# A local and summary attention with mixed experts on one core: band mask in three forms, key maxima in fp16 steps, copies between tiles also as transfers, a new written-out order

## The chip, the cores and the metric

One core of a Trainium2 chip runs the whole program. The time is device time in microseconds for one execution; a lower time is better. Results come as the median over runs, and one further execution was profiled.

## The reference

Two stages follow each other. The first is an attention in which each position sees its neighbours within 15 places and, beside them, 24 summaries of the whole sequence: per block of 32 positions the maximum of the keys and the mean of the values. The second takes the first one's output as `x` and runs four experts, each a causal attention of its own with a projection behind it, mixed by the two strongest gates of each position.

```python
B, H, S, D = q.shape                       # 4, 8, 768, 64
block, window = (32, 16)
k_sum = k.reshape(B, H, nb, block, D).max(axis=3)
v_sum = v.reshape(B, H, nb, block, D).mean(axis=3)
scores_l = scale * np.matmul(q, k.transpose(0, 1, 3, 2))
mask_l = np.abs(pos[:, None] - pos[None, :]) < window
scores_s = scale * np.einsum('bhsd,bhnd->bhsn', q, k_sum)
scores_s = scores_s + np.log(block)
scores_l_m = np.where(mask_l, scores_l, -1000000000.0)
...
a = a / (np.sum(a, axis=-1, keepdims=True) + 1e-09)
v_all = np.concatenate([v, v_sum], axis=2)
return np.matmul(a, v_all).astype(np.float32)
```

```python
logits = x @ w_gate                        # x: (4, 768, 512)
...
for e in range(E):                         # 4 experts, width 64
    q = x @ wq[e]
    k = x @ wk[e]
    v = x @ wv[e]
    ...
    ye = a @ v @ wo[e]                     # a: causal softmax
    for kk in range(K):                    # the 2 strongest gates
        mask = topk[:, :, kk] == e
        out += mask[..., None] * w[:, :, kk:kk + 1] * ye
```

## The kernel before

The work is a list of small steps. `make_plan` makes the list: each step has a name, the buffers it reads and writes, and a function that issues its instructions. `TABLE` holds the order: one entry per step with its number, its engine (V VectorE, A ScalarE, G GpSimd, S SyncE, P TensorE) and the slots of the buffers that it is first to use. `Plan.emit` walks through the table and issues the steps, so the order on each engine's queue is the table's order read for that engine. An engine works through its queue in order: a step that waits holds all behind it. The costs beside each step ("V": 0.95 and so on) and the `dma` figures belong to the planner that made the table; they have no part in the execution. The names in this document are those of the steps, with the batch first, then the head pair or expert pair, then a part: `sc031` is batch 0, head pair 3, half 1.

**Loads.** `dk`/`dq` bring keys and queries of four heads, cast to fp16, on GpSimd's queue; batch 0's first four heads come in two parts. `dv` brings the values of a head pair into `vb` (fp32, 25 tiles of 64 rows, shifted by 16 places) on SyncE's or ScalarE's queue. `vb` has six slots, so later loads wait until earlier head pairs are through.

**Value rows.** A band tile needs 96 rows, 64 own ones and 32 of the next tile. `hc` copies those 32 rows from partitions 0..31 to 64..95 within the tile (L166 or L164, the shared copy helpers). `vq` handles the ends of a head: it copies the last 16 rows and zeroes the first 16 of the next head (L288). `vz` and part of `vone` zero rows and ones once, at the start. `ds` copies the 24 value means, one copy for each of the 12 tiles of a head, into rows 96..119.

**Means.** For batch 0 and some groups `bs` sums with matmuls (L306) and `be` takes the sums out on VectorE (L324). For the groups in `TREE` a second load `dvs` (four DMAs on SyncE, L341) brings the values into `vt`, and `tr` adds them in five steps on GpSimd (L355). `vtz` clears `vt` once ahead of this (L238).

**First stage, per head pair.** `tk`, `tq` transpose keys and queries on TensorE (L373), `kw` lays the keys out in 12 overlapping tiles, `rk` takes the block maxima with one reduction on VectorE (L393), `ksc` copies them into each tile, `cq` takes the queries out. `sc` opens each half with the band mask, a matmul of `mt` with `pi` for each of two heads (L426), and adds the scores (L432). `ex` is the exponential on ScalarE (L440), `av` the matmuls with `vb` (L450), `rc` (L461) and `xm` (L465) divide, `tx` transposes (L477), `hi` and `lo` (L495) split the result into two fp16 parts.

**Second stage, per batch.** `pp` projects (L640), `pc` takes it out, `vp` gives expert values and gates (L570, L573), `lg`/`v2` take them out, `ga`, `gx`, `gb`, `gc` make the gates, `sp` the scores (L664), `es` the exponentials (L672), `dm` the causal cut of diagonal blocks on GpSimd (L677), `aw` the matmuls with the values (L688), `r2` and `wv` weight them, `tw` and `ct` transpose them, `op` projects out (L750), `oc` copies to `ob`, `od` stores (L766). `dw`, `dwv`, `dwo`, `dwg` load weights, `cw`, `cvg`, `cg`, `co` cast them. `f` entries of the table are matmuls on zeros (L773) without any use for the result.

Of the kernel before, what the change touches and what calls it, by code (L numbers as in the profile page):

```python
# [8 lines left out]
HALF = mybir.dt.float16  # L9
# [16 lines left out]
TREE = {(1, 1), (2, 0), (2, 1), (3, 0), (3, 1)}  # L26
# [26 lines left out]
4,V, 18,S,0 10,G, 8,V, 17,V, 0,V, f,P,0.8 7,V, 112,S, 20,A, 13,G,0 15,G, 14,G,0 16,G, 30,G,1 11,G, 1,G, 61,P,1  # L53
5,V, 62,A,0 63,V,0 44,P,0 64,V, 45,A,1 f,P,2.5 31,G,1 78,P,0 79,A,2 9,G, 2,G, 3,V, 46,V,0 65,P,2 48,P,3 99,P,0
204,G,0 49,V,0 82,P,1 66,A,1 24,S,1 19,V, 205,G,2 47,A, 32,S,2 21,P,3 80,V,0 22,V,0 6,G, 52,P,4 83,A,2 81,A,
50,P,1 53,A,0 95,P,6 100,A,0 246,P,7 51,A,1 96,V,1 97,V,0 26,V, 98,G, 229,P,3 67,P,4 68,A,2 25,G, 224,S,0 69,P,0
250,P,2 251,V,1 84,P,4 70,A,3 230,A,0 23,G, 216,G,0 86,P,0 33,G, 27,P,6 28,V,1 87,A,4 247,A,2 85,A,5 248,V,0
34,A, 55,P,0 231,V,1 54,P, 29,G, 56,V,0 103,P,4 104,A,1 35,P,6 71,P,4 57,V,0 36,V,1 38,S,3 39,G, 58,P,0 59,V,0
37,A, 120,G, 60,V,0 72,P, 73,V,0 74,V,0 89,P,6 88,P, 40,A, 101,P,0 102,A,5 41,P,4 280,P,5 90,V,0 91,V,1 42,V,1
43,V, 232,A, 281,A,1 249,G, 254,P,0 255,A,4 252,P,6 92,P,2 93,A,1 206,S,4 209,S,0 233,P,4 234,V,1 116,S,0 115,S,  # L60
117,S,1 225,G, 94,V,1 263,P,5 113,S, 105,P,0 211,A, 106,P, 253,A,5 107,V,0 108,V,1 235,P,2 236,A,1 114,A, 75,P,6
109,P,0 110,V,2 111,V,2 76,A,3 210,G, 208,G, 207,G, 77,V,3 221,S,2 212,P,2 213,V,1 122,G, 264,A,2 166,P,3
168,P,0 217,G,2 119,A, 167,A,0 226,G,0 218,S,3 12,G, 121,A, 169,V,1 227,G, 127,P,6 129,V,0 179,P,0 180,A,0
282,V,1 128,V,0 265,V,0 182,P,2 183,A, 130,P,4 132,A, 124,P,0 214,G, 125,A, 385,S,0 283,V, 131,V, 126,A, 176,P,2
170,P,6 171,A, 267,P,4 139,P,0 133,V,5.0 134,A, 177,A, 223,V, 268,V,0 140,V,2 228,G, 237,P,6 284,P,4 238,A,3
215,G, 266,G, 285,V,1 269,P,2 173,P,0 270,A,2 172,G, 240,P,6 135,V, 136,V,0 239,P, 174,A, 271,P,2 272,A,1 118,S,
123,A, 185,P,0 137,P,4 286,P,2 186,A, 287,A,3 241,V,0 242,V,1 243,P,6 288,P,0 138,V,0 150,P,4 222,V, 289,A,0
257,P,2 244,V,0 245,V,0 151,A,1 220,G, 144,P,0 378,G,2 256,P, 258,V,0 259,V,1 377,G,0 424,P,4 425,V,1 145,A,
386,G, 403,P,5 404,A,1 379,A,0 290,P,0 291,P, 156,P,4 157,A, 147,P,2 260,P,6 261,A,1 390,G,1 219,G, 181,G,
274,P,4 273,P, 148,A, 184,G, 292,V,0 293,V,0 262,V,1 153,P,0 154,A, 275,V,0 276,V,1 187,G, 565,G,1 294,P,2  # L70
295,A,2 632,P,6 296,V,2 387,G,0 392,S,1 437,P,7 277,P,4 278,A,3 149,G, 146,G, 155,G, 279,V,3 420,P,0 407,P,1
559,S,0 566,S,3 421,V,2 438,A,0 408,A,0 339,P,2 340,A,1 341,P,4 178,G, 388,G, 391,G,2 158,G, 175,G, 141,P,2
633,A,2 190,P,0 188,P, 342,A,0 189,P, 346,P,4 422,V,0 423,G, 352,P,6 564,G,0 389,V,2 405,V,0 380,G, 142,A,
191,V,0 192,V,0 406,V, 300,P,2 347,A,0 143,G, 303,P,4 382,A, 301,A,0 302,V,1 381,G, 152,G, 193,P,0 353,A, 305,A,
# [80 lines left out]
def make_plan(nc, T, q, k, v, moe_w_gate, moe_wq, moe_wk, moe_wv, moe_wo, out):  # L155
# [18 lines left out]
    def pbank16(b):  # L174
        return T["ps16"][:, b.slot, :]

    id16, id32, rid, mt, pi = st("id16"), st("id32"), st("rid"), st("mt"), st("pi")
    vones, vz, kwpad, v2one, knpad = st("vones"), st("vz"), st("kwpad"), st("v2one"), st("knpad")
    wqk, wvg, wo = [st("wqk0"), st("wqk1")], st("wvg"), st("wo")

    def id16s(e):
# [753 lines left out]
```

## Time and profile before

| what | us |
|---|---|
| median of 3 runs | 178.65 |
| the three runs | 178.45, 178.65, 183.42 |
| the profiled execution | 177.54 |
| its span, first to last instruction | 175.8 |
| mean granted TensorE clock | 0.956 |
| SyncE waiting to issue an output store behind ScalarE, 5 times | 48.5 |
| GpSimd waiting for exponentials before `dm`, 11 times | 25.1 |

The engines are PE (TensorE's matmuls), PEld (its weight loads, which overlap), DVE (VectorE), ACT (ScalarE), POOL (GpSimd) and SP (SyncE). A row of the groups by line names the line, the engine, the operation, its output and input tile with partitions x elements, the count, then the busy us and mean ns of one, then the idle time of the engine just before, with what ended it. A row of the timeline gives the start and length in us, and in brackets how long the engine was idle before and who released it. The chain of waits follows back from the last instruction to what released each step. Matmuls are pipelined, so the busy time of one is longer than its pitch. The DMA share counts overlapping packets and can exceed 1.

### The profile page before, as it was taken

To read this page: it belongs to the slowest core of one execution; us is meant where nothing else is said; L and a number is where in the kernel's file an instruction comes from. 1 tells how busy PE (TensorE), PEld (TensorE's weight loads), DVE (VectorE), ACT (ScalarE), POOL (GpSimd) and SP (SyncE) were. 2 spreads that over 40 slices of the span, in tenths; PEclk is the share of its full clock that TensorE was granted. 3 is DMA by queue.
4 is the path that set the end of the run, shared out by engine and by line. 5 is a ranking of instruction groups with operands and counts; after the bars stand their busy time and mean duration, and the time that the engine had idled before them with its cause. 6 is when DMAs were issued, how large, how long until landed. Compare 5 with 4: busy or idle time off the path is not lost.

```text
span 175.8 us, 6926 instructions
## 1 busy us (share of the span) xinstructions
PE 148.6 (85%) x3005; PEld 108.8 (62%) x3005; DVE 122.7 (70%) x244; ACT 124.9 (71%) x160; POOL 104.9 (60%) x181
## 2 busy tenths in 40 slices
PE   0667973999896999999998899869999999999760
PEld 0236752798764777867755488648765875675420
DVE  6345566579795987799985788872896986277630
ACT  2344686169948986899687977868989583969650
POOL 8962059746965798379959999927978200324100
PEclk9995699579999999999999999999999999999998
DMA  5999999999998699999969938991001502101846
GB/s 94 181 195 198 216 186 148 152 201 193 153 197 228 80 170 188 173 194 171 150 106 175 181 55 191 250 248 49 4 4 62 183 4 75 44 4 35 300 157 229
DMA packets 44894, 25.60 MB, mean 146 GB/s; under 512 B 33344, under 2 KB 39744, under 8 KB 44864
## 3 DMA queue, kind: packets, MB, share of 16 engines
q1 hardware_dynamic: 33200, 16.08, 47.7%
q0 software_dynamic: 6432, 6.29, 23.5%
q10 hardware_dynamic: 5232, 2.79, 7.7%
q8 instruction: 23, 0.38, 1.0%
q14 instruction: 7, 0.06, 0.1%
HBM read 25.16 MB, written 6.29 MB: 179 GB/s over the span
## 4 chain that ended last, share of the span: by engine, by line
PE 42%; DMA 24%; ACT 10%; POOL 8%; DVE 7%; issue 6%; POOLq 0%; ACTq 0%; DVEq 0%
DMA vb<-in_v_dram 11%; PE ps L450 9%; DMA kn<-in_k_dram 8%; PE ps L640 6%; DMA qn<-in_q_dram 5%; PE ps L570 4%; PE ps L688 4%; ACT a L672 3%; PE ps L664 3%; PE ps L750 3%; PE ps L477 3%; PE ps L373 3%; POOL vb L166 3%; PE ps L306 2%; PE ps L426 2%
## 5 line engine op out<-in xcount | busy, mean ns | idle before, releaser
L672 ACT ACTIVATE a<-ps 128x1024 f16<-128x1024 f32 (+1 forms) x48 | 42.5, 922 | 5.6 <-PE ps L664 4.0
L677 POOL TENSOR_SCALAR_AFFINE_SELECT a<-a 128x256 f16<-128x256 f16 x48 | 19.1, 421 | 28.4 <-ACT a L672 25.1
L440 ACT ACTIVATE aT<-ps 120x768 f32<-120x768 f32 x32 | 25.4, 815 | 9.1 <-PE ps L432 6.9
L450 PE MATMUL ps<-vb,aT 120*64 120x65 f32 x768 | 28.1, 231 | 3.3 <-issue 2.3
L450 PEld LDWEIGHTS ps<-vb,aT 120*64 120x64 f32 x768 | 25.6, 145 | 6.4 <-issue 4.0
L355 POOL TENSOR_TENSOR vt<-vt 120x1024 f32<-120x1024 f32 (+3 forms) x20 | 24.1, 1205 | 1.0
L640 PE MATMUL ps<-hi,wqk 128*128 128x384 f16 x128 | 22.6, 326 | 0.4 <-DVE lo L495 0.3
L166 POOL COPY vb<-vb 16x128 f32<-16x128 f32 (+1 forms) x20 | 14.1, 712 | 9.7 <-DMA vb<-in_v_dram 8.9
L164 ACT COPY kw<-ps 128x1152 f16<-128x1152 f16 x13 | 14.4, 1122 | 7.5 <-PE ps L373 7.5
L393 DVE TENSOR_REDUCE ks<-kw 128x24 f16<-128x768 f16 x16 | 14.9, 943 | 4.8 <-ACT kw L164 4.5
L640 PEld LDWEIGHTS <-wqk 128*128 128x128 f16 x128 | 11.9, 97 | 8.4 <-issue 1.2
L664 PE MATMUL ps<-qk,qk 64*128 64x512 f16 (+3 forms) x128 | 15.8, 307 | 1.0 <-DVE wT L166 0.7
L570 PE MATMUL ps<-wvg,hi 128*128 128x264 f16 x96 | 13.9, 275 | 3.0 <-ACT a L672 1.5
L465 DVE TENSOR_TENSOR x<-ps,rec 128x768 f32<-128x768 f32 x16 | 15.3, 958 | 1.0 <-PE ps L477 0.5
L495 DVE TENSOR_TENSOR lo<-ps,hi 128x768 f16<-128x768 f32 x16 | 15.0, 955 | 1.5 <-ACT hi L164 1.0
L166 POOL COPY vb<-vu 24x768 f32<-24x768 f32 x18 | 14.8, 823 | 1.0
L688 PE MATMUL ps<-v,a 128*128 128x65 f16 x336 | 12.3, 194 | 0.6 <-POOL a L677 0.6
L688 PEld LDWEIGHTS <-a 128*128 128x128 f16 x336 | 11.2, 97 | 2.3 <-issue 0.9
L750 PE MATMUL ps<-wo,wT 128*128 128x512 f16 x48 | 12.0, 380 | 0.5 <-DVE wT L166 0.5
L432 PEld LDWEIGHTS <-kw 64*128 64x128 f16 x384 | 10.4, 98 | 2.8 <-issue 0.7
L426 PE MATMUL ps<-pi,mt 64*128 64x384 f16 x64 | 11.4, 345 | 0.3 <-DVE qT L166 0.3
L432 PE MATMUL ps<-qT,kw 64*128 64x64 f16 x384 | 11.5, 195 | 0.0
(106 smaller groups left out, 269.7 us busy)
## 6 DMA issues: line engine op xcount, KB each, us to landing
vb<-in_v_dram SPq DMA_DIRECT2D x12, 400.0 KB
out_dram<-ob SPq DMA_DIRECT2D x8, 512.0 KB
vt<-in_v_dram SPq DMA_DIRECT2D x20, 192.0 KB
kn<-in_k_dram POOLq DMA_DIRECT2D x7, 384.0 KB, 7.6
qn<-in_q_dram POOLq DMA_DIRECT2D x7, 384.0 KB, 6.3
out_dram<-ob ACTq DMA_DIRECT2D x3, 512.0 KB
vb<-in_v_dram ACTq DMA_DIRECT2D x2, 400.0 KB
vb<-in_v_dram SPq DMA_DIRECT2D x2, 384.0 KB
```

The lines of the kernel that those rows point to most:

```text
L166: en(e).tensor_copy(dst, src)
L355: en(e).tensor_tensor(y, p, q_, AL.add)
L432: nc.tensor.matmul(s[:, hp, 64 * t:64 * t + 64], T["kw"][kw.slot][r, tt, :], T["qT"][qT.slot][r].rearrange("c (s p) -> c s p", s=8)[:, :, ...
L440: nc.scalar.activation(T["aT"][aT.slot][0:KR], pbank(sc, 2)[0:KR, :, 0:384], AF.Exp, scale=SCALE)
L450: nc.tensor.matmul(pbank(av, 2)[o:o + 64, u, 65 * (2 * (t // 2) + hp):65 * (2 * (t // 2) + hp) + 65], a[0:KR, hp, 64 * t:64 * t + 64], T[" ...
L570: nc.tensor.matmul(p[:, i, 0:264], hi_(ch)[:, cols], T["wvg"][:, ch, :], start=(ch == 0), stop=False, skip_group_check=True)
L640: nc.tensor.matmul(pbank(pp, 2)[:, u, 0:384], T["wqk"][:, cc, ch, j, :], hi_(ch)[:, 384 * u:384 * u + 384], start=(ch == 0), stop=(ch == N ...
L664: nc.tensor.matmul(pbank(sp, 2)[:, ep, c0:c0 + w], T["qk"][qk[1].slot][r, 128 * tj:128 * tj + 128], T["qk"][qk[0].slot][r, n0:n0 + w], sta ...
L672: nc.scalar.activation(a2v(u), pbank(sp, 2)[:, :, 0:ln], AF.Exp, scale=SCALE / (XS * XS))
L677: nc.gpsimd.affine_select(m, m, [[0, 2], [1, 128]], AL.is_ge, 0.0, base=0, channel_multiplier=-1)
L688: nc.tensor.matmul(pbank(av, 2)[:, ep, 65 * ti:65 * ti + 65], a2v(u)[:, ep, o:o + 128], T["v2"][v2.slot][:, tj, 2 * cc + ep, :], start=(tj ...
L750: nc.tensor.matmul(pbank(op, i1 - i0)[:, ti - i0, :], T["wT"][wTs[cc].slot][:, 128 * ti:128 * ti + 128], T["wo"][:, cc, :], start=(cc == 0 ...
```

## The change

**Ends of a head.** `vz` and `vq` go, and with them the zeroing in `vone`. The mask tile `mt` gets three forms: the plain band, one with the first 16 columns blocked and one with the last 16. Each `sc` step opens with two mask matmuls for each head instead of one: the first (or last) of its six tiles takes the special form. `hc` now copies rows for all 24 tiles.

**Transfers.** `hc` and `ds` may be issued on SyncE's queue as DMAs: `hc` then reads its rows from the input in device memory, `ds` copies from tile to tile. The table puts five `hc` (10, 22, 23, 30, 31) and three `ds` (12, 23, 33) there.

**Key maxima.** `rk` is three halving `max` steps in fp16 and a reduction over four.

**Others.** Batch 0's second group of keys and queries also comes in two parts, and each part is waited for by itself. Group (1,1) leaves `TREE`: a pair sum `bs12`/`be12` takes the place of its tree load and adds. An assertion in `dv` looks at the slot's history and issues nothing.

**Order.** The whole table is new. Among its moves: `vtz` from GpSimd to VectorE behind `rk03`; `kwz` and `v00` to GpSimd; `id32` and one part of `dk01` behind `mt`; `dv03`, `dv00`, `dv02`, `dv10`, `dv13`, `dv32` and `dwv` to ScalarE's queue, `dv20` and `dv21` to SyncE's; `dvs20` to second place on SyncE's queue; `cvg` to GpSimd, `cw0` to VectorE; fewer `hc`, `ds`, `oc`, `v2` and more `hi` on ScalarE; eight `oc` instead of five on VectorE; five fill matmuls instead of thirteen.

```diff
-TREE = {(1, 1), (2, 0), (2, 1), (3, 0), (3, 1)}
+MT3 = 3
+TREE = {(2, 0), (2, 1), (3, 0), (3, 1)}
...
-4,V, 18,S,0 10,G, 8,V, 17,V, 0,V, f,P,0.8 7,V, 112,S, 20,A, 13,G,0 15,G, 14,G,0 16,G, 30,G,1 11,G, 1,G, 61,P,1
...
+0,V, 22,S,0 4,V, 12,G,0 15,G,0 27,G,1 14,G, 1,G, 36,A,1 30,G,1 28,G, 13,G, 5,G, 41,P,0 42,A,0 16,G,2 75,P,1 2,G,
...
     def masks(e):
         nc.gpsimd.memset(T["mt"], 0.0)
         for h0 in (0, 64):
...
+            w = T["mt"][h0:h0 + 64, :, 0:WIN]
+            nc.gpsimd.affine_select(w, w, [[0, MT3], [-1, WIN]], AL.is_ge, NEG, base=31,
+                                    channel_multiplier=1)
+            nc.gpsimd.affine_select(w, w, [[0, MT3], [1, WIN]], AL.is_ge, NEG, base=-1,
+                                    channel_multiplier=-1)
+        nc.gpsimd.memset(T["mt"][:, 1, 0:16], NEG)
+        nc.gpsimd.memset(T["mt"][:, 2, 80:WIN], NEG)
...
-        en(e).memset(t[0:16, :, 0:24:NQ, 64:65], 0.0)
-        en(e).memset(t[64:96, :, NQ - 1:24:NQ, 64:65], 0.0)
-        en(e).memset(t[64:80, :, NQ - 1:24:NQ, 64:65], 1.0 / XS)
...
-    def vzero(e):
-        t = T["vball"]
-        en(e).memset(t[64:96, :, NQ - 1:24:NQ, 0:64], 0.0)
...
-        def ends(e):
-            w = T["vb"][vb[b, c].slot]
-            copy(e, w[64:80, NQ - 1:24:NQ, 0:64], w[0:16, NQ:25:NQ, 0:64])
-            en(e).memset(w[0:16, 0:24:NQ, 0:64], 0.0)
...
         def edge(e):
             w = T["vb"][vb[b, c].slot]
-            copy(e, by_head(w[64:96, 0:24, 0:64])[:, :, 0:NQ - 1, :],
-                 by_head(w[0:32, 0:24, 0:64])[:, :, 1:NQ, :])
...
+            n = 24 if (b, c) != (B - 1, NCH - 1) else 23
+            if e == "S":
+                nc.sync.dma_start(out=w[64:96, 0:n, 0:64], in_=rows(48, 32, 64, n))
+                if n < 24:
+                    nc.sync.dma_start(out=w[64:80, n:24, 0:64], in_=rows(2 * S - 16, 16, 64, 1))
+            else:
+                copy(e, w[64:96, 0:24, 0:64], w[0:32, 1:25, 0:64])
...
+                if e == "S":
+                    for h in range(2):
+                        nc.sync.dma_start(
+                            out=T["vb"][vb[b, c].slot][WIN:KR, NQ * h:NQ * h + NQ, 0:64],
+                            in_=T["vs"][t.slot][WIN:KR, i, 64 * h:64 * h + 64].unsqueeze(
+                                1).to_broadcast((NSUM, NQ, 64)))
+                    return
...
         def rk(e):
-            nc.vector.tensor_reduce(T["ks"][ks.slot].rearrange("c (t i) -> c t i", i=2),
-                                    T["kw"][kw.slot][:, :, PE0:PE0 + 64].rearrange(
-                                        "c t (i j) -> c t i j", j=32), AX.X, AL.max)
+            w = T["kw"][kw.slot][:, :, PE0:PE0 + 64].rearrange("c t (i j) -> c t i j", j=32)
+            y = T["kt"].rearrange("c (t i) j -> c t i j", i=2)
+            nc.vector.tensor_tensor(y, w[:, :, :, 0:16], w[:, :, :, 16:32], AL.max)
+            y = T["kt"]
+            nc.vector.tensor_tensor(y[:, :, 0:8], y[:, :, 0:8], y[:, :, 8:16], AL.max)
+            nc.vector.tensor_tensor(y[:, :, 0:4], y[:, :, 0:4], y[:, :, 4:8], AL.max)
+            nc.vector.tensor_reduce(T["ks"][ks.slot], y[:, :, 0:4], AX.X, AL.max)
...
             def scs(e, u=u, sc=sc):
                 s = pbank(sc, 2)
-                for hp in range(2):
-                    r = slice(64 * hp, 64 * hp + 64)
-                    nc.tensor.matmul(s[:, hp, 0:384], T["mt"][r, :], T["pi"][r],
-                                     start=True, stop=False, skip_group_check=True)
+                for m, t0, t1 in (((1, 0, 1), (0, 1, 6)), ((0, 0, 5), (2, 5, 6)))[u]:
+                    for hp in range(2):
+                        r = slice(64 * hp, 64 * hp + 64)
+                        nc.tensor.matmul(s[:, hp, 64 * t0:64 * t1], T["mt"][r, m, :],
+                                         T["pi"][r, t0:t1], start=(t0 == 0), stop=False,
+                                         skip_group_check=True)
...
-            load_qk(b, g, 2 if (b, g) == (0, 0) else 1)
+            load_qk(b, g, 2 if b == 0 else 1)
...
-    one("mt", (128, 128), HALF)
+    one("mt", (128, MT3, 128), HALF)
...
+    one("kt", (128, NSUM, 16), HALF)
```

147 lines of the change are left out of this document (78 added, 69 removed).

## The prediction

> **What bounds the kernel now.** I read the page's busy shares first, then the busy time by stage, then the chain of waits and the waits of TensorE.
>
> ```profile
> PE 148.6 (85%) x3005; PEld 108.8 (62%) x3005; DVE 122.7 (70%) x244; ACT 124.9 (71%) x160; POOL 104.9 (60%) x181
> ```
>
> By its share TensorE (PE) comes first, but a mean over the span says little. The busy time by stage cuts it at the kernel's turns: 48 us is the first projection matmul (L640), near 118 us the last loads are in, at 165 us the last attention matmul is done. Each row has the stage, its length, busy us (instructions) of each engine, the granted clock, the DMA share and GB/s.
>
> ```profile
> core 0: us, PE busy (x) PEld busy (x) DVE busy (x) ACT busy (x) POOL busy (x), PEclk, DMA share, GB/s
> 0.00:48.00 48.00, 34.70 (x775) 26.61 (x775) 29.85 (x58) 28.53 (x32) 29.37 (x63) 0.86 1.13 174
> 48.00:118.00 70.00, 64.00 (x1350) 47.62 (x1347) 57.77 (x106) 55.58 (x75) 54.65 (x78) 1.00 1.02 172
> 118.00:165.00 47.00, 46.34 (x860) 33.16 (x859) 31.86 (x72) 37.57 (x51) 20.90 (x41) 1.00 0.17 59
> 165.00:175.80 10.80, 3.54 (x26) 1.36 (x24) 3.24 (x10) 3.19 (x5) 0.00 (x0) 0.92 0.62 228
> ```
>
> From 48 to 165 us TensorE is busy 110.3 of 117 us at full clock, so there the order of its work is the bound and at most 6.7 us of waiting can go. Before 48 us it is idle 13.3 us and its clock is 0.86; after 165 us it is nearly done, and a chain of small steps and output transfers is left. So the change has three places to act: the start, the 6.7 us, and the end. Work taken from GpSimd or ScalarE is worth only what it frees of these.
>
> **The start (term A).** From the timeline (start, us, engine, line), as the marks:
>
> ```profile
> 0.82 0.74 SPq L277 DMA_DIRECT2D vb<-in_v_dram  x1
> ...
> 5.10 1.83 POOL L238 MEMSET vt<- 128x2080 f32 x1
> ...
> 5.73 1.36 ACT L164 COPY vb<-vb 32x1408 f32<-32x1408 f32 x1 [3.63 <-DMA vb<-in_v_dram]
> ...
> 7.77 0.67 POOL L249 DMA_DIRECT2D qn<-in_q_dram  x1
> ...
> 19.33 0.50 PE L426 MATMUL ps<-pi,mt 64*128 64x384 f16 x2
> ...
> 31.64 0.23 DVE L461 RECIPROCAL rec<-ps 128x12 f32<-128x12 f32 x1 [2.09 <-PE ps L450]
> ```
>
> From the chain of waits (start, us, what), the turn into the projections and two loads that the chain passes through, and from the groups by line (busy us, mean ns) the steps that VectorE has before it:
>
> ```profile
> 46.65 1.46 PE ps L306 x48
> 48.10 2.71 PE ps L640 x16
> ...
> 80.47 10.98 DMA vb<-in_v_dram
> ...
> 108.08 7.88 DMA vb<-in_v_dram
> ```
>
> ```profile
> L465 DVE TENSOR_TENSOR x<-ps,rec 128x768 f32<-128x768 f32 x16 | 15.3, 958 | 1.0 <-PE ps L477 0.5
> L495 DVE TENSOR_TENSOR lo<-ps,hi 128x768 f16<-128x768 f32 x16 | 15.0, 955 | 1.5 <-ACT hi L164 1.0
> ...
> L393 DVE TENSOR_REDUCE ks<-kw 128x24 f16<-128x768 f16 x16 | 14.9, 943 | 4.8 <-ACT kw L164 4.5
> ...
> L164 ACT CAST hi<-ps 128x768 f16<-128x768 f32 x11 | 8.7, 799 | 2.6 <-PE ps L477 2.4
> ...
> L166 DVE COPY qT<-ps 128x768 f16<-128x768 f16 x11 | 6.1, 552 | 2.6 <-PE ps L373 2.2 <-issue 0.3
> ```
>
> In the old order GpSimd issues its sixth q/k load only at 7.77 us, behind id32 and the 1.83 us clearing of vt (L238), and the first scores (L426) come at 19.33 us. In the new one seven half-size q/k loads leave GpSimd first (about 0.7 us each, from 0.8 us), two v loads instead of three with four tree loads go beside them, and the clearing of vt moves to VectorE, behind rk03. VectorE's chain then sets the first scores: hc01 on ScalarE (1.36 us, as at 5.73) lies between kw00 and kw02, which I put done near 10.3 us, and then three rk (2.8 us), cq00 (0.55) and v2o, pi, be01 and ksc00 (some 2.8 together, my estimate) stand ahead of the scores. I put the first scores at 16.5 us, 2.8 us earlier, and the first normalisation (L461) at 28.8 instead of 31.64 us. Not all of TensorE's queue goes with it: tk11 waits for dk100, which GpSimd now issues only behind hc00, which waits for dv00; sc010, tk10 and av000 are queued behind tk11. The old order had stalls of its own there, so I count these equal.
>
> From the first normalisation VectorE has four rc and xm, cq10, rk10, two lo and a ksc before tx03 can run. With 0.23 + 0.96 a pair, 0.55, 0.94, 1.91 and about half a us that is 8.7 us, so tx03 stands at 38 us instead of just ahead of 46.65. be03, ds03 and three of the hi copies, which lay on VectorE in the old stretch, are earlier or on other engines. Here a new wait arises: **dv10** was issued by SyncE near 18 us. Now ScalarE issues it behind hi03, near 38.8 us, and bs10, which needs its rows, stands in TensorE's queue ahead of every projection matmul. So the projections start at 38.8 us plus one v load plus 1.46 us. The three rows above give the load as 4.9 us (0.82 to 5.73), 7.88 and 10.98 us; that is 45.2, 48.1 or 51.2 us against 48.10. I take 4.9: ScalarE's queue is empty by then, as SyncE's was in the first row, while the two others were taken with tree loads and q/k loads in front. The Trainium skill (DMA: Bandwidth & Descriptors, Anatomy of one DMA) fits one DMA as 2.0 us plus bytes over 436 GB/s, 2.9 us for these 400 KB; no load in this trace comes near it, and by it the sum would be 2.0 us lower, 171.9 us, still inside the forecast's own range below.
>
> ```profile
> 13.19:17.58 4.39, 3.26 (x76) 3.07 (x78) 2.30 (x6) 2.15 (x3) 0.90 (x3) 0.56 1.22 198
> ...
> 30.77:35.16 4.39, 4.39 (x79) 3.50 (x75) 2.33 (x6) 0.81 (x1) 3.24 (x4) 0.50 1.01 152
> ```
>
> These two stages, cut at slices of the page, are the ones behind the long idle stretches of TensorE in the start. The new wait leaves TensorE idle some 5 us; behind those stretches the clock was 0.56 and 0.50 for a slice of 4.4 us. I add 1.7 us for it, a little under half such a slice. The Trainium skill (TensorE: Matmul & The Clock Gate, Part 1) has the same against this order: an idle window of about 3.4 us halves the clock until a busy window of that length has passed, 1.7 us by its figure. A = -2.9 + 1.7 = **-1.2 us**, with ends -3.9 (no clock loss, and the key maxima at the low price worked out under C, -1) and +4.9 (10.98 us).
>
> **More matmuls (B).**
>
> The weight loads of the mask matmuls, and twelve score matmuls in the chain of waits:
>
> ```profile
> L426 PEld LDWEIGHTS <-mt 64*128 64x128 f16 x64 | 3.4, 95 | 3.8 <-issue 2.9
> ```
>
> ```profile
> 104.46 0.19 PE ps L432 x12
> ```
>
> The mask takes four matmuls instead of two in each of 32 score steps, over the same 384 columns. Twelve 64-column matmuls take 0.19 us in the chain, 16 ns each, so two more cost between nothing (the columns are the same) and 0.03 us, and 0.19 us if both weight loads lay open: 0, 1.0 or 6.1 us in all. I take 0.5, near the chain's pitch, because weight loads are covered almost everywhere. (1,1) leaves the tree, so bs12 adds 48 matmuls, 1.46 us by the row at 46.65, inside the stretch that TensorE sets. B = **+2.0 us** (1.5 to 7.6). The eight fill matmuls that go ran while TensorE had nothing else: 0.
>
> **Waits in the middle (C).**
>
> TensorE's waits between 48 and 165 us (engine, line, whom it waited for, us, times, longest), then the groups that the change takes from:
>
> ```profile
> PE ps L570 <- ACT a L672: 1.5, 1, 1.5
> PE ps L570 <- ACT qk L164: 1.3, 1, 1.3
> ...
> PE ps L664 <- DVE wT L166: 0.7, 1, 0.7
> PE ps L688 <- POOL a L677: 0.6, 1, 0.6
> ```
>
> ```profile
> L164 ACT COPY vb<-vb 32x1408 f32<-32x1408 f32 x5 | 6.8, 1365 | 5.9 <-DMA vb<-in_v_dram 5.8
> L355 POOL TENSOR_TENSOR vt<-vt 120x1024 f32<-120x1024 f32 (+3 forms) x20 | 24.1, 1205 | 1.0
> ...
> L166 POOL COPY vb<-vb 16x128 f32<-16x128 f32 x12 | 3.4, 286 | 7.5 <-DMA vb<-in_v_dram 7.1
> ```
>
> Four waits of TensorE from 48 to 165 us, 4.1 of the 6.7 us, hang on engines that the change relieves. ScalarE's 1.5 us comes where it holds two v2 copies beside the exponentials; v2 goes to VectorE. Its 1.3 us comes behind hc30, which stands on ScalarE until the load lands and then copies 1.37 us; hc30 is now a transfer. VectorE's 0.7 us follows its copy hc22, also a transfer now, and GpSimd's 0.6 us follows hc21, which waited for its rows. In all GpSimd loses twelve vq (3.4 us of copies, and a clearing each), one tree of five (24.1/5 = 4.8 us), four ds and one hc, against three ksc, cvg and a longer mt. ScalarE loses four hc (5.5 us), one ds, three oc, two v2. VectorE gains: two ds, three oc, three v2, be12, vtz and cw0 against four vq, vz and some copies, about 5 us net; it was busy 57.8 of 70 us, and that slack is the cover. If it is gone, the 4.1 us come back.
>
> For the key maxima the nearest groups of VectorE are these:
>
> ```profile
> L716 DVE TENSOR_TENSOR wav<-ps,cmb 128x512 f16<-128x512 f32 x2 | 1.4, 692 | 0.1
> L716 DVE TENSOR_TENSOR wav<-ps,cmb 128x256 f16<-128x256 f32 x2 | 0.8, 424 | 0.1
> L621 DVE TENSOR_TENSOR gs<-gs,ps 128x24 f32<-128x24 f32 x4 | 0.7, 173 | 0.1
> ```
>
> The key maxima become four instructions over 384, 192, 96 and 96 elements. At the slope of the two L716 rows (1.05 ns an element, 0.16 us fixed) they take 1.4 us, at the price of four tiny ones (L621) 0.7, against the 0.94 of L393. I take no change: the operands are half as wide as in L716, and each of four starts costs. The ends are -0.25 and +0.5 us a head pair; on the start's chain that counts some four times, -1 to +2.
>
> SyncE's queue gets five hc and three ds transfers, 5,568 packets of 256 B, and loses one tree load. The loads end by 118 us with 47 us of matmuls still to come, and none of the four waits above is TensorE's for a load, so I cost the bytes at nothing there. Three waits stand ahead of others in that queue: dvs20 for vtz, with dv11, three weight loads and hc10 behind it; ds12 for be12, with dv31, dv20 and dv21 behind it; od020 for oc020, with dv23, hc23, hc31 and ds23. They are covered as long as those loads are used later than they land. C = **-4.1 us** (0 to -6).
>
> **The end (D).** The timeline's last attention and output matmuls, and the copy of two output tiles on VectorE:
>
> ```profile
> 163.29 1.44 PE L688 MATMUL ps<-v,a 128*128 128x65 f16 x42
> ...
> 167.71 2.48 PE L750 MATMUL ps<-wo,wT 128*128 128x512 f16 x10
> ```
>
> ```profile
> L166 DVE COPY ob<-ps 128x1024 f32<-128x1024 f32 x3 | 3.7, 1222 | 1.7 <-PE ps L750 1.7
> ```
>
> From the last attention matmul (164.73 us) to the end are 11.1 us. The old order first finishes the last two tiles, then starts the four others (r2310). The new one starts those four when aw310 and aw311 are done, with op21 (four output matmuls, 1.0 us at 2.48/10) and aw312 (22 of 42 matmuls, 0.75 us) behind them: 1.7 us sooner, and without r2311 and wv311 in front (0.4 us for wav alone). Against it oc310, oc320 and oc330 stand in a row on VectorE, 1.22 us and then some 1.1 for the tile and a half after it, where oc310 alone was last: 1.1 more. The last transfer is 128 KB instead of 512, which I count as 0.5 us. 1.7 + 0.4 - 1.1 + 0.5: D = **-1.5 us** (-2 to +1.5).
>
> **Sum.** -1.2 + 2.0 - 4.1 - 1.5 = -4.8 us. The profiled execution took 177.54 us (1.7 us around its span), 1.1 below the median of the three runs; from 177.54 it becomes 172.7, and on the median's footing 178.65 - 4.8 = **173.9 us**, 2.7% faster.
>
> **Rivals.** *Late first rows of batch 1.* Either dv10 takes the 10.98 us row, or hc10 lands that late: before it in SyncE's queue lie 2.2 MB, held by vtz, and at 174 GB/s those alone take 12.5 us. A becomes +4.9 and the time 180.0; the middle values (7.88 us) give 177. For it: the stretch to 48 us has a DMA share of 1.13. Against: fewer loads are in flight at that time than in the old order.
>
> *ScalarE held by its own DMA issues (the slower side).* It now issues six v loads and one weight load instead of two and one.
>
> ```profile
> L277 SPq DMA_DIRECT2D vb<-in_v_dram x14: 595/664/6307, 0.8 to 110.7; - x14
> L277 ACTq DMA_DIRECT2D vb<-in_v_dram x2: 603/642/682, 68.6 to 80.5; - x2
> ```
>
> SyncE stood 6.3 us at one issue where its queue was full; ScalarE never did with its two. If dwv meets dv00 and dv02 still queued, ScalarE stands 5.6 us with kw03 and the exponentials behind it, all on the way to 48 us. One held issue makes 179.5; two make 185.1, so from the second it is slower by over 2%.
>
> *Gains beyond the sum.* The clock kept and cheap key maxima (A = -3.9), masks at nothing (B = 1.5) and the low end of D (-2): 170.2. *The waits do not go*, because VectorE takes over as the late engine: C = 0, 178.0.
>
> **How the numbers follow.** Forecast 0.45 (its own range 171.5 to 175); gains beyond 0.08 (169 to 171.5); late rows or waits that stay 0.28 (175 to 181.5); ScalarE held 0.19 (181.5 to 186). Two per cent, 3.6 us, is about what a measurement of this kernel can tell from no change, as its three runs span 178.45 to 183.42. Faster by over 2% (below 175.1) 0.53, within 0.28, slower 0.19. The range 169.0 to 181.5 leaves out the held ScalarE and little else.
>
> **What would show it.** A: the first L640 matmul near 47 us with a TensorE wait for a vb load right before it and a clock near 0.5 after. B: TensorE about 2 us busier from there to the last attention matmul. C: no wait of L570 on ScalarE over 1 us. D: under 10 us from the last L688 to the end. Wrong it would be if the ScalarE queue shows issues of several us, if TensorE's idle time in the middle stays at 6 us, or if the projections start after 50 us.

## The result, and the profile after

The changed kernel takes 205.24 us (median of 4 runs, 204.46 to 208.37) against 179.27 us for the kernel before on the same chip: the ratio is 1.1446, with an interval of 1.1358 to 1.1534. The forecast was 173.9 us, in a range of 169.0 to 181.5. It is wrong in sign and far outside.

The profiled execution of the changed kernel has a span of 202.7 us, 26.9 more than before. First, the busy shares and the first line of the chain of waits on its page:

```profile
PE 154.6 (76%) x3109; PEld 114.1 (56%) x3109; DVE 141.7 (70%) x291; ACT 116.3 (57%) x149; POOL 90.2 (45%) x148
...
PE 38%; DVE 29%; DMA 12%; ACT 7%; issue 7%; POOL 3%; SPq 2%; DVEq 0%; ACTq 0%; POOLq 0%
```

GpSimd lost 14.7 us of work and ScalarE 8.6, as the change meant; VectorE gained 19.0, and 29% of the chain that ended last now lies on it. Where the time went shows in the busy time by stage, cut at the same turns: first projection matmul (now L665), last attention matmul, end. The first three rows are the changed kernel.

```profile
0.00:59.23 59.23, 34.66 (x790) 27.60 (x790) 35.68 (x72) 25.75 (x30) 28.98 (x54) 0.84 1.02 149
59.23:191.50 132.27, 116.44 (x2295) 85.02 (x2292) 101.31 (x210) 88.25 (x116) 61.27 (x94) 0.96 0.60 112
191.50:202.70 11.20, 3.51 (x36) 1.49 (x32) 4.75 (x10) 2.29 (x4) 0.00 (x0) 0.90 0.64 233
```

The middle of the kernel before, for the same cut:

```profile
48.04:164.73 116.69, 110.03 (x2202) 80.62 (x2200) 89.43 (x177) 93.04 (x124) 75.50 (x119) 1.00 0.68 126
```

The start is 11.2 us longer (59.23 against 48.04), the middle 15.6 (132.27 against 116.69), the end 0.1. In the middle TensorE is idle 15.8 us instead of 6.7, and its matmuls are busy 116.44 us instead of 110.03, at a granted clock of 0.96 instead of 1.00. The start ends in a wait for a load: these are pieces of the chain of waits, with the first projection right behind them.

```profile
47.76 8.49 DMA vb<-in_v_dram
...
56.39 2.93 PE ps L310 x48
```

`dv10` was issued at 47.76 us and `bs10` (L310) could start only when it had landed. In the middle the list of TensorE's waits has new names:

```profile
PE ps L665 <- DVE v L166: 4.6, 1, 4.6
PE ps L502 <- DVE x L490: 3.0, 1, 3.0
PE ps L665 <- DVE lgp L166: 1.9, 1, 1.9
...
PE ps L713 <- DVE wav L741: 1.6, 1, 1.6
```

The four waits that the prediction counted are gone, but for 0.2 us on GpSimd; 11.1 us on VectorE stand in their place. What VectorE did meanwhile is in its groups by line: the four steps of the key maxima, `rk`, took 30.2 us against 14.9 for the one reduction before.

```profile
L415 DVE TENSOR_TENSOR kt<-kt 128x192 f16<-128x192 f16 x16 | 12.4, 773 | 0.6
L416 DVE TENSOR_TENSOR kt<-kt 128x96 f16<-128x96 f16 x16 | 7.1, 443 | 0.6
L413 DVE TENSOR_TENSOR kt<-kw 128x384 f16<-128x384 f16 x16 | 6.7, 421 | 8.7 <-ACT kw L164 8.5
L417 DVE TENSOR_REDUCE ks<-kt 128x24 f16<-128x96 f16 x16 | 4.0, 253 | 1.0
```

A step over 192 elements (L415) with a longer mean than one over 384 (L413) cannot be paying for its elements. The single durations by line say more: L415 has 257, 340 and 2290 ns as least, median and most, L416 208, 209 and 1852, while the reduction L417 has 252, 253 and 254. The chain of waits just ahead of TensorE's longest wait, and GpSimd's timeline beside it:

```profile
100.20 0.28 DVE kt L413
...
100.50 2.30 DVE kt L415
...
102.83 1.86 DVE kt L416
...
104.78 0.25 DVE ks L417
105.04 0.61 DVE v L166
...
105.69 2.40 PE ps L665 x7
```

```profile
100.23 2.44 POOL L367 TENSOR_TENSOR vt<-vt 120x1024 f32<-120x1024 f32 x1
102.63 0.69 POOL L249 DMA_DIRECT2D kn<-in_k_dram  x1
103.33 2.61 POOL L367 TENSOR_TENSOR vt<-vt 120x512 f32<-120x512 f32 x3
```

L415 began at 100.50 and ended at 102.8, when GpSimd's add of 2.44 us (100.23 to 102.67) had ended; L416 stood until 104.7 beside the next adds. `v` comes behind them on VectorE, and the projections behind `v`. In a pause of GpSimd, from 13.51 to 14.68 us, the same four steps took 0.36, 0.26, 0.21 and 0.25 us. The reduction `ks` (L417) ran beside GpSimd's adds from 104.78 us and took its 0.25 us. Of the 48 steps with two operands all 16 that took 0.40 us or more ran beside a GpSimd instruction. So theory 1 of the experiments is: a VectorE step with two operands in SBUF waits for the GpSimd instruction then running, that makes the new maxima long, and with the late `dv10` it makes most of the 26.9 us. Its rivals: the new order is worse as a whole, the mask's matmuls cost more than thought, or the transfers hold SyncE's queue.

### The profile page after: what moved, and what is told of

Read it like the earlier page. It is cut to its first block, busy times and chain, and to the rows that moved or that the text cites. A ratio compares the mean times of both kernels' runs of the same rounds, so it can differ in the third digit from the quotient of the medians.

```text
span 202.7 us, 7144 instructions
## 1 busy us (share of the span) xinstructions
PE 154.6 (76%) x3109; PEld 114.1 (56%) x3109; DVE 141.7 (70%) x291; ACT 116.3 (57%) x149; POOL 90.2 (45%) x148
## 4 chain that ended last, share of the span: by engine, by line
PE 38%; DVE 29%; DMA 12%; ACT 7%; issue 7%; POOL 3%; SPq 2%; DVEq 0%; ACTq 0%; POOLq 0%
PE ps L665 8%; PE ps L475 6%; DVE kt L415 5%; PE ps L713 4%; DMA vb<-in_v_dram 4%; DMA kn<-in_k_dram 4%; ACT a L697 3%; PE ps L502 3%; DVE kt L416 3%; PE ps L310 3%; PE ps L595 3%; DMA a<-in_moe_wo_dram 3%; PE ps L390 3%; DVE x L490 2%; PE ps L775 2%
## 5 line engine op out<-in xcount | busy, mean ns | idle before, releaser
L665 PE MATMUL ps<-hi,wqk 128*128 128x384 f16 x128 | 26.0, 358 | 6.6 <-DVE v L166 4.6
L475 PE MATMUL ps<-vb,aT 120*64 120x65 f32 x768 | 26.9, 224 | 1.9 <-issue 1.5
L665 PEld LDWEIGHTS <-wqk 128*128 128x128 f16 x128 | 12.9, 106 | 17.4 <-issue 11.5
L164 ACT CAST qk<-ps 128x768 f16<-128x768 f32 x11 | 8.7, 801 | 20.8 <-PE ps L665 20.2
L367 POOL TENSOR_TENSOR vt<-vt 120x1024 f32<-120x1024 f32 (+3 forms) x16 | 20.0, 1248 | 0.9
L390 PE MATMUL ps<-rid,kn 98*64 98x98 f16 (+1 forms) x256 | 10.6, 233 | 12.6 <-DMA kn<-in_k_dram 10.0
L166 POOL COPY vb<-vs 24x1536 f32<-24x1536 f32 x6 | 9.2, 1534 | 24.0 <-DVE vs L328 24.0
L310 PE MATMUL ps<-vb,sel 80*32 80x128 f32 x192 | 10.5, 383 | 9.7 <-DMA vb<-in_v_dram 7.9
L390 PEld LDWEIGHTS <-kn 98*64 98x64 f16 (+1 forms) x256 | 8.3, 126 | 14.1 <-issue 13.5
L713 PE MATMUL ps<-v,a 128*128 128x65 f16 x336 | 14.0, 202 | 1.9 <-DVE wav L741 1.6
L520 DVE TENSOR_TENSOR lo<-ps,hi 128x768 f16<-128x768 f32 x16 | 14.9, 952 | 0.2
L166 POOL COPY vb<-vb 32x1536 f32<-32x1536 f32 x7 | 10.3, 1478 | 9.0 <-DMA vb<-in_v_dram 8.7
L310 PEld LDWEIGHTS ps<-vb,sel 80*32 80x32 f32 x192 | 7.7, 152 | 10.6 <-issue 8.0
```

The costliest lines, as they stand in the source:

```text
L164: nc.scalar.copy(dst, src)
L166: en(e).tensor_copy(dst, src)
L310: nc.tensor.matmul(pbank(sp)[32 * j:32 * j + 32, 0, 0:128].rearrange("p (h d) -> p h d", h=2), T["sel"][:, 22 - 2 * tt:54 - 2 * tt], T["vb ...
L367: en(e).tensor_tensor(y, p, q_, AL.add)
L390: nc.tensor.matmul(dst[64 * hp:64 * hp + 64, c0:c0 + eye.shape[-1]], src[0:n, hh + hp, 64 * s:64 * s + 64], eye, is_transpose=True)
L475: nc.tensor.matmul(pbank(av, 2)[o:o + 64, u, 65 * (2 * (t // 2) + hp):65 * (2 * (t // 2) + hp) + 65], a[0:KR, hp, 64 * t:64 * t + 64], T[" ...
```

## The experiments

Every kernel ran beside the kernel before on the same chip, and a ratio is always to that. The times of different rows come from different chips, on which the kernel before took 179.17 to 181.31 us (medians), so small differences between rows are to be taken from the ratios. Turns are read from each kernel's trace as above: `first` is the first projection matmul, `middle` from there to the end of the last attention matmul (in the changed kernel 191.45 us, just ahead of the cut above).

| kernel | us, median | ratio (interval) | first | middle |
|---|---|---|---|---|
| the changed kernel | 205.24 | 1.1446 (1.1358 to 1.1534) | 59.2 | 132.2 |
| with the old maximum | 193.26 | 1.064 (1.0557 to 1.0723) | 58.1 | 121.5 |
| with `dv10` early | 195.55 | 1.0769 (1.0657 to 1.0881) | 53.2 | 129.0 |
| with both | 185.06 | 1.0294 (1.0179 to 1.0409) | 49.7 | 121.5 |
| with GpSimd's instructions cut | 197.84 | 1.0984 (1.0877 to 1.1091) | 61.0 | 123.3 |
| cut, and `dv10` early | 187.35 | 1.0533 (1.0427 to 1.0638) | 50.5 | 122.3 |
| cut, `dv10` early, old maximum | 188.27 | 1.0487 (1.0325 to 1.0649) | 49.7 | 123.5 |

### The old maximum in the changed kernel

```diff
-            nc.vector.tensor_tensor(y, w[:, :, :, 0:16], w[:, :, :, 16:32], AL.max)
-            y = T["kt"]
-            nc.vector.tensor_tensor(y[:, :, 0:8], y[:, :, 0:8], y[:, :, 8:16], AL.max)
-            nc.vector.tensor_tensor(y[:, :, 0:4], y[:, :, 0:4], y[:, :, 4:8], AL.max)
-            nc.vector.tensor_reduce(T["ks"][ks.slot], y[:, :, 0:4], AX.X, AL.max)
+            nc.vector.tensor_reduce(T["ks"][ks.slot].rearrange("c (t i) -> c t i", i=2),
+                                    T["kw"][kw.slot][:, :, PE0:PE0 + 64].rearrange(
+                                        "c t (i j) -> c t i j", j=32), AX.X, AL.max)
```

> The changed kernel with the old key maxima, one reduction a head pair. Theory 1 (the key maxima): the four steps took 30.2 us of VectorE in the changed kernel against 14.9 us before, 1.08 us where GpSimd stands still and up to 4.9 us where it works; VectorE has become the engine that TensorE waits for, so 10 to 16 us come back: 189 to 195 us. Theory 2 (the order: late loads and late first scores): less than 4 us come back, over 201 us.

It takes 193.26 us, ratio 1.064: by the medians 12.0 us less. The middle shrinks from 132.2 to 121.5 us and TensorE's waits of 4.6, 3.0 and 1.9 us for VectorE are gone, so nearly all of it comes from there. The start hardly moves, although the first normalisation comes at 34.64 instead of 38.48 us: `dv10` is issued at 45.91 us instead of 47.76, and lands at 55.14.

### The new maximum in the kernel before

The same edit the other way round, in the old order.

> The kernel before with the new key maxima alone, same order. Theory 1: VectorE loses 5 to 15 us there too, 183 to 193 us. Theory 2: VectorE has slack in the old order, at most 2 us more: under 181.5 us.

185.0 us, ratio 1.0167 (1.0069 to 1.0264): some 3 us. The groups are longer here too, 26.0 us in all against 14.9 (the profile is of the longest of the four runs, 188.68 us), so the effect does not need the new order; most of the price does. Two of them:

```profile
L395 DVE TENSOR_TENSOR kt<-kw 128x384 f16<-128x384 f16 x16 | 8.4, 524 | 4.7 <-ACT kw L164 4.5
L397 DVE TENSOR_TENSOR kt<-kt 128x192 f16<-128x192 f16 x16 | 7.3, 457 | 0.6
```

In the old order eleven microseconds more of VectorE cost about three. In the new one, where TensorE stands behind VectorE, fifteen more cost twelve.

### `dv10` issued early

Entry 203 (`dv10`) moves on ScalarE's queue from behind `hi03` (107) to right behind `dwv` (114), and into the slot of `vb` that is free by then.

```diff
-114,A,0 201,G,0
+114,A,0 203,A,5 201,G,0
...
-107,A,2 203,A,1 204,S,
+107,A,2 204,S,
```

> The changed kernel with dv10 issued early on ScalarE's queue, right behind dwv, into the sixth value buffer, so that bs10 need not wait for it. Theory 2: the 7.9 us wait of TensorE ahead of the first projection goes and the clock is kept: 195 to 199 us. Theory 1: VectorE is late there anyway, at most 3 us come back: 202 us or more.

195.55 us, by the medians 9.7 less than the changed kernel. `bs10` starts at 50.36 us instead of 56.39. With the old maximum as well:

> The changed kernel with both: the old key maxima and dv10 issued early. Alone they gave back 12 and 9.7 us of 26. If the two are separate (VectorE's added time all along, and one wait at 48 us), they add up: 183 to 186 us. If they are two sides of one delay, they give less than 15 us together: 190 us or more.

185.06 us. By the medians the two repairs take 20.2 us together, one by one 12.0 and 9.7, so they add up. By the ratios they take 0.115 together and 0.081 and 0.068 one by one, so a fifth of what they give alone may be common to both. Either way each gives what the other does not, so they are two causes, not one. What the start waits for next is another transfer; the chain of waits has, in the kernel with both:

```profile
43.01 4.40 DMA vb<-in_v_dram
...
47.46 2.31 PE ps L310 x39
```

That is `hc10`, a transfer in the new order: it stands in SyncE's queue behind the tree load, `dv11` and four weight loads, was issued at 43.01 us and landed at 47.41.

### GpSimd's instructions cut short

The maxima stay as in the change. GpSimd's copies of 24 blocks and its adds over 1024 and 512 elements become two, four or more instructions for the same data:

```diff
-                copy(e, w[64:96, 0:24, 0:64], w[0:32, 1:25, 0:64])
+                for k_ in range(4 if e == "G" else 1):
+                    m = 6 if e == "G" else 24
+                    copy(e, w[64:96, m * k_:m * k_ + m, 0:64],
+                         w[0:32, m * k_ + 1:m * k_ + m + 1, 0:64])
...
-                    en(e).tensor_tensor(y, p, q_, AL.add)
+                    if w == 1024:
+                        for h_ in range(2):
+                            for c0 in (0, 256):
+                                en(e).tensor_tensor(y[:, h_, c0:c0 + 256], p[:, h_, c0:c0 + 256],
+                                                    q_[:, h_, c0:c0 + 256], AL.add)
...
```

> The changed kernel with GpSimd's long instructions cut up: its copies of 24 blocks and its tree adds of 1024 and 512 elements are each made as two to four shorter ones, and nothing else is changed. Theory (a VectorE step with two SBUF operands waits until the GpSimd instruction then running has ended): the four key-maximum groups fall from 30.2 us to 20 to 23 us (17 us if none waited), the longest step of the second group from 2.29 to under 1 us, and the time by some microseconds, to 198 to 204 us. Rival (these steps are slow for a reason of their own, or GpSimd holds VectorE off over a whole run of instructions): the groups stay near 30 us, with the same two kinds of duration, and the time stays within 2 us of 205.

Nothing that VectorE does was touched, and its four groups fell from 30.2 to 21.7 us:

```profile
L433 DVE TENSOR_TENSOR kt<-kw 128x384 f16<-128x384 f16 x16 | 6.8, 424 | 9.1 <-ACT kw L164 8.9
L435 DVE TENSOR_TENSOR kt<-kt 128x192 f16<-128x192 f16 x16 | 5.9, 367 | 0.6
L436 DVE TENSOR_TENSOR kt<-kt 128x96 f16<-128x96 f16 x16 | 5.0, 312 | 0.6
L437 DVE TENSOR_REDUCE ks<-kt 128x24 f16<-128x96 f16 x16 | 4.0, 253 | 1.0
```

The longest step of the second group is 668 ns now, not 2290, and the time is 197.84 us, by the medians 7.4 less (ratio 1.0984 against 1.1446). It is less although the first projection comes 1.8 us later than in the changed kernel (`dv10` was issued at 47.47 and landed at 58.06): the middle has fallen to 123.3 us, nearly as far as the old maximum took it. Two more kernels close the square, both with `dv10` early:

> The changed kernel (new key maxima) with dv10 issued early and GpSimd's instructions cut short. With long instructions this kernel took 195.6 us, and with the old maximum as well 185.1: the new maxima cost 10.5 us there, for 13.0 us more of VectorE (27.9 against 14.9). Theory (most of that price is the wait for GpSimd's running instruction, and it adds to the late load): with short ones the groups stay near 21.7 us, 6.8 more than the old, and the time is 186 to 190 us. Rival (the price is the four steps themselves, however long GpSimd's are): 193 to 196 us.

> The changed kernel with the old key maximum, dv10 issued early and GpSimd's instructions cut short. Theory (the cut helps through the key maxima, which are not in this kernel; GpSimd is busy some 9 us longer by the cuts): within 2 us of the 185.1 us that it takes with long ones, so that the new maxima cost 3 to 6 us at short instructions against 10.5 at long ones. Rival (the cut helps in another way, say by GpSimd's own steps coming in a finer order): 178 to 182 us here too, and the price of the maxima stays near 10 us.

The first takes 187.35 us and the second 188.27. In whole instructions the new maxima cost a ratio of 0.0475 (1.0769 less 1.0294); in cut ones 0.0046, which is less than the two intervals can tell from nothing (together they leave some 0.02 either way). The second missed its expectation, within 2 us of 185.1: it is 3.2 above, so cutting alone is no gain and perhaps a loss, for GpSimd is busy 97.2 us in it against 90.3. The groups of the maxima in the first sum to 20.4 us against 15.1 for the reduction in the second. Five microseconds more of VectorE without long waits cost nothing that can be measured. By the medians, cutting took 8.2 us off the kernel with the new maxima, out of the 10.5 that they cost there, and put 3.2 on the kernel with the old one. So most of the price was VectorE's waits and not its work; that the difference closes wholly lies in part in the second kernel, which the cuts made longer.

### The mask in three forms alone

The kernel before, in its order, with the change to `masks`, `sc` and `hc`, without `vq` and `vz`:

```diff
-                    nc.tensor.matmul(s[:, hp, 0:384], T["mt"][r, :], T["pi"][r],
-                                     start=True, stop=False, skip_group_check=True)
+                for m, t0, t1 in (((1, 0, 1), (0, 1, 6)), ((0, 0, 5), (2, 5, 6)))[u]:
...
-        R.step(f"vq{b}{c}", {"G": 0.45, "V": 0.35}, [vr[b, c], vz], [vb[b, c], vs_[b, c]], ends)
```

> The kernel before with the band mask in three forms alone: the zeroing and the copies at the ends of a head go, two more mask matmuls stand in each of 32 score steps, the order is kept (two value buffers swap slots). My term for the mask (0.5 us) with 5.8 us of GpSimd work gone: 177 to 180 us. Rival: the weight loads of the added matmuls lie open (6.1 us): 184 us or more.

182.1 us beside 181.31: no difference that can be told. It lies between the two cases expected, so neither came. TensorE is busy 149.7 us instead of 148.6, so the 64 matmuls more cost at most about 1.1 us of it (the granted clock was 0.950 against 0.956), and no gain shows from GpSimd's 3.5 us less (101.4 against 104.9) in this order.

### Transfers instead of copies

In the kernel with both repairs, the five `hc` and three `ds` that were transfers become GpSimd copies again (eight entries, as 385, `hc23`):

```diff
-385,S,
+385,G,
```

> As e5_max_load, and the five hc and three ds that are transfers on SyncE's queue are copies on GpSimd, in the same places of the order. If the transfers hold SyncE's queue or load the DMA engines where TensorE waits, 2 to 5 us come back against e5_max_load. If they take work from GpSimd as meant, it is 2 to 5 us slower; between them they did not matter.

194.35 us, 9.3 more on the same chip, and more than expected. TensorE's waits between 40 and 185 us are now these:

```profile
PE ps L390 <- DMA kn<-in_k_dram: 5.3, 2, 4.4
PE ps L470 <- POOL vb L166: 4.6, 3, 2.7
PE ps L390 <- DMA qn<-in_q_dram: 3.3, 1, 3.3
```

The longest wait for `kn` comes in the same way as the wait for a copy: GpSimd issues that load behind its copies, at 68.43 us instead of 63.58 in the kernel with both repairs, and it landed at 77.23. The wait for `qn` does not: that load was issued earlier (60.23 against 61.20) and took 9.7 us instead of 7.8, and what made it longer is open. So in the new order the transfers pay. In the old order, in the kernel with the mask alone, `hc22`, `hc23`, `hc30` and `hc31`, each right behind its load on SyncE's queue (`hc22` for one, which is 382 in the table of that kernel):

```diff
-382,V,
+382,S,
```

> The kernel before with the mask in three forms (its order kept) and with four of the group copies (hc22, hc23, hc30, hc31) made as transfers on SyncE right behind the loads that they copy. Theory (the transfers are the part of the change that pays, because they free GpSimd and VectorE where their late steps are waited for): 2 to 4 us less than the same kernel with copies, 177 to 180 us. Rival (in the old order these copies are hidden, and a transfer only lengthens SyncE's queue): within 1 us of it, or 1 to 3 us more.

181.2 us, ratio 1.0078 (1.0018 to 1.0138): the gain did not come. TensorE's longest wait there is for ScalarE, with 3.4 us at one place:

```profile
PE ps L566 <- ACT a L668: 3.4, 1, 3.4
PE ps L684 <- POOL a L673: 1.7, 1, 1.7
```

### Two more moves in the kernel with both repairs

`vtz`, the clearing that the tree load waits for, went back to GpSimd behind `dk011`, so that the tree load leaves early (the first line of the diff). In another kernel `dv23`, `hc23` and `hc31` moved on SyncE's queue ahead of `dvs31` (556), which waits there for `vt` (the second).

```diff
+29,G, 10,G,
...
+386,S,0 384,S,3 385,S, 544,S,
```

> As e5_max_load, and the clearing of vt goes back to GpSimd, behind dk011, so that VectorE loses 1.8 us near 30 us and dvs20 with all behind it on SyncE's queue is issued some 15 us earlier. If that queue sets the first projection and the weights, 2 to 5 us come back against e5_max_load; if not, within 1 us of it.

> The changed kernel with the old key maximum and the early load of dv10, as run before at 185.1 us, with dv23, hc23 and hc31 moved on SyncE's queue ahead of dvs31, which holds the queue for 21.7 us there. Theory (SyncE's held queue makes what remains against the kernel before): 1 to 4 us less, 181 to 184 us. Rival (what remains is in the start and in TensorE's own added work): within 1 us of 185.

Both missed. The first takes 189.89 us, 4.8 more: the tree load left at 15.11 us instead of 29.85, and among TensorE's waits before 52 us there is now one for a copy of VectorE, `hc02`, which stood until its load had landed: the early tree load had come in front of the loads of batch 0. ScalarE also stood 3.79 us at the issue of `dv10` (from 24.99 us).

```profile
PE ps L390 <- DMA kn<-in_k_dram: 10.3, 2, 9.6
PE ps L310 <- DVE vb L166: 6.0, 2, 5.8
```

The first row, up to 9.6 us for keys, is no longer than without the move; the second was 0.9 us there.

The second takes 187.2 us (183.9 to 188.71). Its four runs lie too far apart for a ratio, and the shortest is no better than the kernel with both repairs (184.24 to 188.76). No gain shows; that the queue, held for 21.7 us there, holds nothing that is needed soon is likely by this, but a small gain is not excluded.

## Why the prediction was wrong

**A, the start: forecast -1.2 us, measured +11.2.** The working had the first normalisation at 28.8 us, `tx03` at 38, `dv10` issued at 38.8 and landed 4.9 us later. The trace has 38.48, 46.70 and 47.76 us, and 8.49 us for the load. From the first normalisation to the issue the 10.0 us of the sum were right (9.3 measured); the failed step is what stands ahead of it, and it has three parts. The first is the first keys. The sum had `kw00` and `kw02` done near 10.3 us; they were done at 13.47. The first key load, issued at 1.37 us, took 7.31 us, and the first one before, issued at 1.70, took 4.93. So the first mask matmul came at 19.58 us instead of 16.5, no earlier than in the old order (19.33). Why that load was slower was not tried.

```profile
9.72 1.12 ACT L164 COPY kw<-ps 128x1152 f16<-128x1152 f16 x1 [6.87 <-PE ps L390]
10.86 1.47 ACT L164 COPY vb<-vb 32x1536 f32<-32x1536 f32 x1
...
12.35 1.12 ACT L164 COPY kw<-ps 128x1152 f16<-128x1152 f16 x1
...
19.58 0.34 PE L450 MATMUL ps<-pi,mt 64*128 64x320 f16 x4
```

The second part is the key maxima, taken at no change: the old maximum brings the first normalisation forward by 3.8 us (34.64 against 38.48). The third is `tk11` and the keys of the second group, which GpSimd issues only behind `hc00`: the working named this chain and then counted it equal to the stalls of the old order. With the old maximum the chain of waits runs through just this load, issued at 21.88 us, 5.86 us long, with `tk` behind it at 27.78 us.

The second error is the size of the load. "ScalarE's queue is empty by then" was true and of no use: while the load ran the other queues moved data too, at a DMA share of 1.38, and it took 8.5 us (47.76 to 56.25), and 9.2 with the old maximum (45.91 to 55.14) and 10.6 with the cut instructions (47.47 to 58.06). All three lie between the middle and the upper of the three rows that the working had. In those rows the share was 0.87 at 4.9 us, 1.14 at 7.88 and 1.16 at 10.98, so the lowest was the row with the least traffic; the share does not order the others, and no run varied it alone. The Trainium skill (DMA: Bandwidth & Descriptors, Anatomy of one DMA) states the fit of 2.0 us plus bytes over 436 GB/s for loads that GpSimd issues; of those, with 384 KB each, the shortest in the trace before took 4.9 us.

Of the excess over the 45.2 us that these steps gave, 9.0 us are the issue, 3.6 the load and 1.5 `bs10` at half pace, 2.93 us instead of 1.46. This last is the clock loss, forecast at 1.7.

**B, more matmuls: forecast +2.0 us, right.** In the changed kernel itself the lower clock hides it. In the kernel with both repairs, at a granted clock of 0.99, TensorE is busy 1.9 us longer in the middle than before:

```profile
49.69:171.20 121.51, 111.97 (x2292) 82.35 (x2292) 90.73 (x180) 88.14 (x116) 61.77 (x94) 0.99 0.71 126
```

That is 111.97 against 110.03. The parts met the sum less closely: the mask's was up to 1.1 us in its own kernel, where 0.5 was taken, and the new `bs12` takes 1.53 us in the timeline of the kernel with both repairs, where 1.46 was.

**C, waits in the middle: forecast -4.1 us, measured about +9 of idle time.** That the four waits would go was right. Two steps failed. The larger is the cover, "it was busy 57.8 of 70 us, and that slack is the cover", with "I take no change" for the maxima by the slope of two rows whose first operand lies in PSUM. Alone the four steps take 1.08 us against 0.94, within the ends of the working; the wait was the term it put at nothing. A share of busy time says how long an engine could be late in all, not whether a step that TensorE waits for stands behind a step that has become nine times as long for once. The maxima were measured at 30.2 us instead of 14.9, and by the old maximum alone the middle fell by 10.8 us: some 7 us of idle time, and 3.5 of busy time with the clock back from 0.96 to 0.98, a loss that the working had nowhere in the middle. The Trainium skill (SBUF — State Buffer, Who interferes with whom) states the rule that the prediction should have weighed: a VectorE instruction with two inputs in SBUF contends with a GpSimd instruction that reads SBUF, and a reduction never does. The trace agrees on both: up to 2290 ns for L415 beside an add of GpSimd, 252 to 254 ns for all sixteen L417.

The smaller step is that the sum took the four waits off and put none of the new order's own on. With the old maximum the middle reads:

```profile
58.00:179.60 121.60, 112.94 (x2294) 82.75 (x2292) 90.76 (x179) 87.94 (x116) 61.64 (x94) 0.98 0.65 120
```

TensorE is still idle 8.7 us there, and 9.5 in the kernel with both repairs, where the forecast makes 2.6. The longest waits of the latter are 1.9 us for ScalarE and 1.6 for `wav` on VectorE.

**D, the end: forecast -1.5 us, measured +0.1.** The four tiles do start earlier, 2.0 us behind the last attention matmul (193.44 less 191.44) instead of 3.0, but the working left out that `ob` has three slots. The last output tile waits until a store of another has landed, and the store that the chain stands behind took longer than the one in the old order, 3.03 us against 1.73; these pieces of the chain of waits of the changed kernel follow the last output matmul that counts:

```profile
194.56 1.02 ACT ob L164
...
195.60 3.03 DMA out_dram<-ob
...
198.72 0.42 DVE ob L166
```

**The rivals.** "Late first rows" came, by `dv10`; with `dv10` early it came a second time by `hc10`, the other half of that rival, landed at 47.41 us. "The waits do not go, because VectorE takes over" had the right engine and the wrong price: it was given 178.0 us, as if the waits could only stay as they were, and they grew. "ScalarE held by its own DMA issues", the case on which the chance of slower rested, did not happen in the changed kernel: its issues took 0.4 to 1.3 us until `dv10`, and no exponential stood behind one. Two of the signs of being wrong that the prediction names came: the projections started after 50 us (59.2), and TensorE's idle time in the middle did not fall below 6 (15.8).

**What stays.** With both repairs the kernel is still slower than before, by a ratio of 1.0294. By the two profiles (182.5 against 175.8 us) that is 1.7 us in the start, 4.8 in the middle and 0.2 at the end; of the middle 1.9 us are B and 2.9 idle time, spread over waits of which the longest, for ScalarE, is 1.9 us. Two attempts on it, by the tree load and by SyncE's queue, did not find it. That `hc10` makes the rest of the start is read from the chain of waits and was not tried. No version that ran is faster than the kernel before; the parts that were tried alone in the old order came out at no difference that can be told (mask), 0.2 to 1.4% slower (mask with transfers) and 0.7 to 2.6% slower (maxima).

## What to carry to other kernels

Before an instruction on VectorE is replaced by several with two operands in SBUF, look at what GpSimd runs beside it: here each of them could wait for GpSimd's whole instruction, a reduction over one operand did not, and shorter GpSimd instructions gave most of the time back. An engine's slack as a share of its time covers nothing by itself; look at which step TensorE waits for and what stands ahead of it in that queue. A load's duration is to be taken from rows with the same traffic, not from a row with an empty queue of the same engine: here 4.9 us at a DMA share of 0.87 became 8.5 at 1.38.

## What the runs showed of the hardware

The size of the wait was not expected: a step of 0.26 us became 1.40 us beside a GpSimd copy and 2.29 us beside an add. It isn't only steps with two operands. VectorE's own copy of 24 blocks within a tile (`hc`) takes 0.95 us alone and 2.18 us at 21.31 us, beside the same copy of another tile on GpSimd:

```profile
21.31 2.18 DVE L166 COPY vb<-vb 32x1536 f32<-32x1536 f32 x1
...
26.41 0.95 DVE L166 COPY vb<-vb 32x1536 f32<-32x1536 f32 x1
```

```profile
21.22 1.46 POOL L166 COPY vb<-vb 32x1536 f32<-32x1536 f32 x1 [1.31 <-DMA vb<-in_v_dram]
```

And GpSimd does not keep VectorE off over a run of instructions: with four copies back to back (1.93 us in all from 99.12 us) the second and third step of a maximum took 0.44 and 0.39 us, so there the wait ended with the instruction that ran, which is why cutting it helps. A step that begins first is not held: the L413 of 18.22 us began 0.12 us ahead of a GpSimd copy and took 0.36. One step of the changed kernel waited for more than the instruction then running: L416 began at 102.83 us beside GpSimd's issue of a load (until 103.32) and ended at 104.68, just behind the first of the adds after it. What held it there is open.
